# A state-space block with a token MLP on one core: norm sums on TensorE, a contiguous lag table, a fifth Strassen pair

## The chip, the cores and the metric

One core of one Trainium2 chip runs the whole kernel. The metric is the device time of one execution in microseconds, the median over several executions. The span in the profile is about 1.8 us shorter than that time. The granted clock is TensorE's clock as the profile shows it, as a share of full speed. Every run here compares with runs of the kernel before on the same chip in the same rounds; "ratio" is the mean time of one kernel's fast runs over the mean of the other's fast runs of those rounds, so it is not quite the ratio of the medians that stand beside it. The kernel before took 155.7 to 159.95 us on the chips used, most often 156 to 158.

## The reference, cut to what matters

```python
def reference(A_u, ..., B_w1, B_b1, B_w2, B_b2):          # x is 2048 tokens by 512 channels, bf16
    x = A_u
    h = x + ssm_conv(layernorm(x), ...)                    # a 2048-tap convolution for each channel
    # per channel: K[l] = Re sum_n C_n * exp(dt*A_n*l) * dt*B_n   (128 modes), y = K conv u + u*D
    return h + token_mlp(layernorm(h), B_w1, B_b1, B_w2, B_b2)
    # token_mlp: u = gelu(h^T @ w1 + b1)  (2048 -> 1792), y = u @ w2 + b2  (1792 -> 2048)
```

## The kernel before

The convolution is split at blocks of 128 tokens. The near part (inside a block and its neighbour) goes through a 64-point spectrum, `UF`. The far part goes through eight Chebyshev nodes for each block: **moments** `ms` of the normed x (a row for each block and node) are written to DRAM and read back as a table `Mb` of all shifts; the **far table** `G` holds the kernel at all lags between nodes; and the **lag product** multiplies the two, for each of 32 channel groups `s` and four quarters `q`. Its first call (O0) serves blocks 0 to 7, its second (O1) blocks 8 to 15. Each is 128 matmuls with 32-column weights.

```python
    def moments(self, hf):                       # hf = half of the blocks
        ...                                      # 8 matmuls into bank 3, then out with the norm's bias
        b.act(self.ms[r0:r0 + 64, :], self.bank(3, 0, D, r0, r0 + 64), AF.Identity, bias=self.mb[...])

    def far(self):                               # G is [P, 16, NJ, 32]: dims x, i (or j), s
        for i in range(0, NJ, 2):
            ...                                  # two matmuls fill two banks: (i, x, s)
            dst = self.G[:, :, i:i + 2].rearrange("p x i s -> p i x s")    # runs of 32 s side by side
            b.ts(dst, src, ...)  or  b.act(dst, src, AF.Copy)              # two on DVE, two on ACT

    def lag(self, hf):
        Gv = self.G[...].rearrange("p (q j) i s -> p q s (j i)", q=4)      # weights: one element every 64 bytes
        Mv = self.Mb[...].rearrange("p k (q j s) -> p q s k j", q=4, j=4)  # moving: likewise
        for s in range(32):
            for q in range(4):
                b.mm(self.ps[32*q:32*q+32, 32*s:32*s+32], Gv[:, q, s], Mv[:, q, s])
```

Behind O1 come the inverse transforms, the second norm and the token MLP, with four Strassen pairs in layer 1 (a pair forms two blocks of output columns with seven matrix products in place of eight). No order is written by hand: a list scheduler in the kernel file sets the order on each engine from a table of priorities, a cost for each instruction and an overlap test of the tiles that it reads and writes.

Other names in the text: an **eviction** copies a result from PSUM, where TensorE writes, to SBUF; `T` are eight products of exponentials and sines on DVE, from which TensorE forms samples of the convolution kernel; `kt` are the samples that G's matmuls read, `kf` those for the near part; `WL` and `nm` carry the weights and bias terms of the first norm; a y chunk is the inverse transforms and the far part of one block, which DVE adds to `X`; `H` is the second norm's output. The pitch is the time from one matmul's start to the next one's, and a filler is a matmul whose result nobody reads.

## Time and profile before

| | kernel before |
|---|---|
| time | 156.7 us (median) |
| span, granted TensorE clock | 154.7 us, 1.00 |
| first and second `ms` handed to the DMA | 26.9, 44.9 us |
| O0 starts, O1 starts | 44.6, 54.4 us |
| TensorE from O1 to its end | 97.9 us |

The groups of instructions, shapes apart, show what the change touches. A line has engine, operation, tiles, count, then busy us in all, the mean ns of one, and the engine's idle time ahead of it. (The 265 ns of one matmul overlap with those of its neighbours: 128 of them take 2.86 us.)

```profile
L499 PE MATMUL ps<-Mb,G 128*32 128x32 bf16 x256 | 5.7, 265 | 0.3 <-DMA Mb<-ms_scratch 0.3
...
L530 DVE TENSOR_SCALAR G<-ps 128x1024 bf16<-128x1024 f32 x2 | 2.4, 1217 | 0.0
...
L506 ACT ACTIVATE G<-ps 128x1024 bf16<-128x1024 f32 x2 | 1.9, 1020 | 0.0
...
L506 ACT ACTIVATE ms<-ps,mb 64x512 bf16<-64x512 f32 x2 | 1.4, 689 | 0.0
```

An eviction of 1024 elements to G takes 1.0 to 1.2 us, 1.0 to 1.2 ns an element, and one of `ms` (512) 0.69 us.

### The profile page before, as it was taken

To read this page: it belongs to the slowest core of one execution; us is meant where nothing else is said; L and a number is where in the kernel's file an instruction comes from. 1 tells how busy PE (TensorE), PEld (TensorE's weight loads), DVE (VectorE), ACT (ScalarE), POOL (GpSimd) and SP (SyncE) were. 2 spreads that over 40 slices of the span, in tenths; PEclk is the share of its full clock that TensorE was granted. 3 is DMA by queue.
4 is the path that set the end of the run, shared out by engine and by line. 5 is a ranking of instruction groups with operands and counts; after the bars stand their busy time and mean duration, and the time that the engine had idled before them with its cause. 6 is when DMAs were issued, how large, how long until landed. Compare 5 with 4: busy or idle time off the path is not lost.

```text
span 154.7 us, 3685 instructions
## 1 busy us (share of the span) xinstructions
PE 143.5 (93%) x1522; PEld 106.7 (69%) x1529; DVE 131.4 (85%) x308; ACT 78.2 (51%) x192; POOL 6.7 (4%) x11
## 2 busy tenths in 40 slices
PE   7849869989998889999999999999999999999993
PEld 3738753568565485545554788888888888888882
DVE  5099999998999998999999999957999994558663
ACT  4897999998997868614544832545320000000000
POOL 1590000000000000000000000000000000000000
PEclk9999999999999999999999999999999999999999
DMA  4899996266992508995590000000000101211123
GB/s 108 264 310 360 406 403 240 65 230 176 417 372 83 202 4 310 419 408 222 166 375 3 0 6 0 0 0 4 0 0 0 38 34 68 71 54 51 66 73 103
DMA packets 12351, 23.64 MB, mean 153 GB/s; under 512 B 1181, under 2 KB 8350, under 8 KB 12206
## 3 DMA queue, kind: packets, MB, share of 16 engines
q1 hardware_dynamic: 12190, 23.27, 41.8%
q8 instruction: 12, 0.20, 0.5%
q10 hardware_dynamic: 144, 0.13, 0.2%
q14 instruction: 5, 0.04, 0.1%
HBM read 21.17 MB, written 2.35 MB: 152 GB/s over the span
## 4 chain that ended last, share of the span: by engine, by line
PE 67%; DMA 14%; DVE 7%; SPq 5%; ACT 3%; issue 2%
PE ps L499 67%; DMA tab<-tables 8%; SPq L556 5%; DMA Mb<-ms_scratch 4%; DVE T L522 3%; DVE cmu L522 3%; DMA ms_scratch<-ms 2%; ACT G L506 1%; DVE ct L522 1%; ACT UF L506 1%; PE ps L784 1%; ACT ms L506 0%; ACT kf L506 0%; DVE X L536 0%; ACT mb L506 0%
## 5 line engine op out<-in xcount | busy, mean ns | idle before, releaser
L499 PE MATMUL ps<-H,W 128*128 128x512 bf16 (+1 forms) x180 | 32.5, 327 | 0.3 <-issue 0.2
L499 PEld LDWEIGHTS ps<-H,W 128*128 128x128 bf16 x184 | 17.7, 98 | 10.6 <-DVE H L532 0.2
L784 PE MATMUL ps<-idf 128*128 128x256 bf16 x162 | 22.0, 282 | 1.0 <-POOL idf L547 1.0
L499 PE MATMUL ps<-gT,W 128*128 128x256 bf16 x182 | 22.6, 273 | 0.0
L499 PEld LDWEIGHTS ps<-gT,W 128*128 128x128 bf16 x182 | 17.0, 98 | 3.0 <-DVE X L522 0.2
L784 PEld LDWEIGHTS ps<-idf 128*128 128x128 bf16 x162 | 15.6, 101 | 4.3 <-POOL idf L547 1.0
L522 DVE TENSOR_TENSOR W<-W 128x1024 bf16<-128x1024 bf16 (+1 forms) x23 | 14.9, 657 | 0.3 <-PE ps L499 0.2
L522 DVE TENSOR_TENSOR X<-ps,acc 128x256 bf16<-128x256 f32 x24 | 10.0, 422 | 5.5 <-PE ps L499 5.2
L499 PE MATMUL ps<-HT,W 128*128 128x256 bf16 x112 | 14.2, 273 | 0.0
L506 ACT ACTIVATE H<-X 128x512 bf16<-128x512 bf16 x16 | 10.0, 624 | 7.7 <-DVE X L536 7.7
L536 DVE SCALAR_TENSOR_TENSOR acc<-ps,b2T,X 128x256 f32<-128x256 f32 x24 | 11.1, 481 | 2.8 <-PE ps L499 2.2
L499 PEld LDWEIGHTS ps<-HT,W 128*128 128x128 bf16 x112 | 10.9, 98 | 1.4
L499 PE MATMUL ps<-TS,S 128*128 128x256 bf16 x84 | 11.6, 273 | 0.0
L499 PE MATMUL ps<-TS,W 128*128 128x256 bf16 x84 | 11.3, 273 | 0.0
L536 DVE SCALAR_TENSOR_TENSOR X<-ps,X 128x512 bf16<-128x512 f32 x16 | 10.6, 687 | 0.2 <-PE ps L499 0.2
L506 ACT ACTIVATE gT<-snap,b1T 128x256 bf16<-128x256 f32 x12 | 6.0, 505 | 9.1 <-DVE snap L522 9.1
L542 DVE BATCH_NORM_STATS2 st<-X 128x6 f32<-128x512 bf16 x12 | 7.4, 679 | 3.5 <-DMA X<-in_A_u_dram 3.5
L506 ACT ACTIVATE UF<-ps,ub 128x512 bf16<-128x512 f32 x16 | 10.2, 686 | 0.2 <-PE ps L499 0.2
L499 PEld LDWEIGHTS ps<-TS,S 128*128 128x128 bf16 x84 | 7.9, 98 | 1.4 <-DVE acc L536 0.4
L499 PEld LDWEIGHTS ps<-TS,W 128*128 128x128 bf16 x84 | 8.2, 98 | 1.0
L506 ACT ACTIVATE gT<-ps,b1T 128x512 bf16<-128x512 f32 (+1 forms) x10 | 5.4, 606 | 4.7 <-PE ps L499 4.7
L499 PEld LDWEIGHTS ps<-O,tab 128*128 128x128 bf16 x64 | 4.8, 98 | 3.9 <-DVE O L530 0.8
(127 smaller groups left out, 233.4 us busy)
## 6 DMA issues: line engine op xcount, KB each, us to landing
W<-in_B_w_dram SPq DMA_DIRECT2D x4, 1792.0 KB, 10.9
W<-in_B_w_dram SPq DMA_DIRECT2D x2, 2048.0 KB, 9.3
W<-in_B_w_dram SPq DMA_DIRECT2D x2, 1536.0 KB, 7.9
Mb<-ms_scratch SPq DMA_DIRECT2D x2, 1024.0 KB, 6.0
out_dram<-X SPq DMA_DIRECT2D x15, 128.0 KB, 1.7
tab<-tables SPq DMA_DIRECT2D x1, 1296.0 KB, 13.1
X<-in_A_u_dram SPq DMA_DIRECT2D x4, 256.0 KB, 4.7
X<-in_A_u_dram SPq DMA_DIRECT2D x2, 512.0 KB, 11.8
```

The lines of the kernel that those rows point to most:

```text
L499: return self.r.add("pe", lambda e: e.matmul(out, lhsT=lhsT, rhs=rhs, start=start, stop=stop, skip_group_check=onto), [lhsT, rhs], [out], ...
L506: return self.r.add("act", lambda e: e.activation(out=out, in_=in_, func=func, bias=bias, scale=scale, accum_out=accum_out), [in_, bias, s ...
L522: return self.r.add(eng, lambda e: e.tensor_tensor(out=out, in0=a, in1=b, op=op), [a, b], [out], self._d(eng, nel(out), m), **k)
L536: return self.r.add(eng, lambda e: e.scalar_tensor_tensor(out=out, in0=a, scalar=s, in1=b, op0=op0, op1=op1, accum_out=accum_out), [a, s, ...
L542: return self.r.add("dve", lambda e: e.bn_stats(out=out, in_=a), [a], [out], 67 + nel(a) / 0.96, **k)
L556: return self.r.add(eng, lambda e: e.dma_start(out=out, in_=in_), [in_], [out], max(by / RATE.get(out.tensor.name.split("_")[0], 410) + 0. ...
L784: self.rec.hot = (hot, lambda e, bk: e.matmul(self.bank(bk, 0, 256), lhsT=hv[:, 0:P], rhs=hv[:, :], start=True, stop=True))
```

## The change

The intent: take the first norm's statistics off DVE (TensorE forms x·x and the row sums from transposed loads of x), put each set of 32 weights of the lag product side by side, work G off in two halves so that O0 can start on the first, save TensorE time by a fifth Strassen pair, and move the scaling of the DFT weights to ACT. All priorities are new. The core of the diff, with cuts:

```diff
-        self.G = take("G", [P, 16, NJ, 32], BF16)
+        self.G = take("G", [P, 2, 16, 16, NJ], BF16)           # half, s, x, j
 def far(self):
+        for h in range(2):
+            for c in range(0, 4, 2):
 ...
-            dst = self.G[:, :, i:i + 2].rearrange("p x i s -> p i x s")
+                    dst = self.G[:, h, :, :, 2*(c+q):2*(c+q)+2].rearrange("p s x i -> p i x s")
+                    src = self.bank(bb + q).rearrange("p (i x s) -> p i x s", i=2, x=16)
+                    # odd ones on DVE, even ones on ACT, 512 elements each
 def lag(self, hf):
-        Gv = self.G[...].rearrange("p (q j) i s -> p q s (j i)", q=4)
-        Mv = self.Mb[...].rearrange("p k (q j s) -> p q s k j", q=4, j=4)
+        Gv = self.G[...].rearrange("p h s (q j) i -> p h q s (j i)", q=4)
+        Mv = self.Mb[...].rearrange("p k (q s j) -> p q s k j", q=4, j=4)
 def moments(self, hf):
-        b.act(self.ms[r0:r0+64, :], self.bank(3, 0, D, r0, r0+64), ...)
+        b.act(self.ms[r0:r0+64, :].rearrange("p (q s j) -> p q j s", q=4, j=4),
+              self.bank(3, 0, D, r0, r0+64).rearrange("p (q j s) -> p q j s", q=4, j=4), ...)
+def stats(self, hf):             # in place of BN_STATS on DVE
+        for k in range(8):       # Gram blocks of 32 tokens: t^T t for 4 channel chunks
+            ... b.mm(self.bank(bk, ...), t, t, ...)
+        ...                      # row sums against a column of ones; mask and reduce on DVE
 def loads(self):
-        ... x in six pieces, W1's quarters 0 and 1 early
+        for h in range(2):
+            ld(17 + h, self.XT[:, h], self.x_in[0][...], transpose=True)
+            ld(8 + h, self.X[:, 8*h:8*h+8], xv[:, 8*h:8*h+8])
+PAIRS = [(6, 10), (7, 11), (8, 12), (9, 13), (4, 5)]           # fifth Strassen pair
+FA = (0,)                                                      # first half's DFT weights scaled on ACT
```

## The prediction

> **What bounds the kernel now.** I read the chain in order of time first: it says which wait ends last at each point.
>
> ```profile
> 9.19 12.65 DMA tab<-tables
> ...
> 25.82 3.68 DVE T L522 x5
> ...
> 39.85 0.34 PE ps L499 x2
> 40.19 0.02 issue
> 40.21 1.94 ACT G L506 x2
> ...
> 44.22 0.70 ACT ms L506
> 44.91 0.02 issue
> 44.93 3.14 DMA ms_scratch<-ms
> 48.07 0.02 issue
> 48.09 6.31 DMA Mb<-ms_scratch
> 54.40 0.04 issue
> 54.44 2.85 PE ps L499 x114
> ...
> 81.83 70.49 PE ps L499 x621
> ```
>
> The columns are start, length and what. Up to 54.4 us the kernel is a chain of latencies: parameters and the T products on DVE, samples and the far table G, then the second half of the moments through DRAM (3.1 us out, 6.3 us back). From 54.4 to 152.3 nothing but TensorE is on it. The busy table by stretches confirms it and shows the second danger:
>
> ```profile
> core 0: us, PE busy (x) PEld busy (x) DVE busy (x) ACT busy (x) POOL busy (x), PEclk, DMA share, GB/s
> ...
> 45.00:54.40 9.40, 7.93 (x158) 5.14 (x152) 9.12 (x20) 7.68 (x20) 0.00 (x0) 1.00 0.49 165
> ...
> 60.00:70.00 10.00, 9.95 (x58) 5.05 (x58) 9.77 (x25) 4.39 (x16) 0.00 (x0) 1.00 1.02 414
> 70.00:82.00 12.00, 11.89 (x77) 6.78 (x78) 11.70 (x30) 6.38 (x20) 0.00 (x0) 1.00 0.63 234
> 82.00:94.00 12.00, 12.00 (x92) 8.90 (x91) 11.59 (x32) 6.14 (x13) 0.00 (x0) 1.00 0.01 3
> ```
>
> From 60 to 94 us TensorE has no gap, but DVE has under 3% left too. So the end is the start of the second lag product (O1, 54.44) plus TensorE's work after it. That work can be counted from the program, with the pitches of the trace (217 ns a 512-column matmul, 109 ns a 256-column one, from runs of 24 in 5.4 us and of 28 in 3.06 us): O1 2.85, twelve y chunks of 0.65, 96 matmuls of the plain half of layer 1 20.8, four Strassen pairs of 56 x 109 ns 24.4, layer 2 (392 x 109 ns) 42.7; sum 98.5. 54.4 + 98.5 = 152.9 against 152.3 seen. The last DVE addition and the output DMA add 2.4 us to the span (154.7), and the time is 1.8 us over the span (156.5 for the profiled run).
>
> **What the Trainium skill says.** "TensorE: Matmul & The Clock Gate", section Back-to-back issue gap: N/2.4 + 2.5 ns warm, 109 ns for 256 columns; the trace agrees. Its section on the 56 ns gap puts a floor of about 25 ns on the start-to-start of small matmuls; the lag product, column-packed, runs 128 in 2.86 us, 22.3 ns each, so the measurement decides. "SBUF — State Buffer", section Door 1, gives 16-byte lines that a stride should stay within; G's weights stand 64 bytes apart now, and 22.3 ns against 13.3 ns of streaming 32 columns at 2.4 GHz is compatible, though not shown to be due to it. "DMA: Bandwidth & Descriptors", section Latency and other measured facts, gives a crossbar transpose 261 GB/s with a non-contiguous middle dimension, 350 to 400 contiguous. No run before shows a transpose; 1 MB is then an estimated 3 to 4 us.
>
> **The change, part by part.**
>
> Norm 1. Removed: 12 BN_STATS at 0.61 us pitch (7.3 us of DVE) and four ACT pairs (5.6 us between 29.7 and 36.6). Added: two transposed loads ahead of x itself, 128 small matmuls and 32 one-column sums for each half, and on DVE a masking pass and a reduction (0.4 us each, twice). The first half's BN_STATS ran at 7.5 to 12.4 us, and m waited behind them, while its own inputs (CX, written at 9.13) were ready by about 9.9. In the new order ACT reaches the sines earlier (square moved behind the table load): I get the last sine at 16.5 us instead of 17.3. DVE's list from SN to the last T is SN 0.74, q 0.6, mask and reduction 0.8, the complex products 8.0 and eight T's of 0.735: about 16. So T ends near 32.3 instead of 35.1: 2.8 us won. Condition: the first transpose is in by about 12 us (0.8 MB of parameters first, done near 6.5, then 4 us, then latency), so that the Gram matmuls end by 17.5 at the cold clock.
>
> G and the order behind T. This is where I see the gain spent. The retuned order puts WL, nm (the norm's bias terms) and the second half's reduction after the last T. The bias, hence every UF eviction and the first moments, waits for them, and bank 5 is shared by the second half's sums and half of the samples. In order: T 32.3; nm 33.5; bias on ACT 34.5; the moments' matmuls 35.6; UF, exponential, UF, ms to 36.6 (0.57 us each with bias); the other samples on PE to 38.5; select 40.4; kt 41; then G. Before, T to kt took 39.1 - 35.1 = 4.0 us, now some 8.5, seven of which are ACT evictions that before ran at 23 to 30 us. G's evictions alternate ACT and DVE but each waits for the one before in the same half (their write ranges interleave): 4 x 0.75. G's first half is ready at 44.5. The moments arrive too: ms 36.6, out 2, back 5.6 (the first pair in the trace: issue 26.88, 28.82): 44.3. O0 therefore starts at about 44.5, against 44.57: **nothing is won up to here**.
>
> The lag product. Contiguous weights: I take 16 ns for 22.3: 0.8 us a half.
>
> O0 to O1. The half of Mb that does not depend on the second ms is fetched early, so the last fetch is 0.5 MB: 3.8 us estimated for 6.3. ms1 comes after O's eight evictions on ACT (2.3), y0, a bias, a UF, an H square: 6 us after O0 starts, at 50.5 to 51. 51 + 2 + 3.8 = 57 for **O1, 2.5 us later than before**. In return eight y chunks and three inverse transforms are done by then, instead of four.
>
> TensorE after O1. Counting the new program: O1 2.0, y 4.6, 64 plain matmuls 13.9, five pairs 30.5 (a pair costs 6.1 for 6.94 plain, so the fifth saves 0.84), layer 2 42.7: 93.7 to 95. Saved: 4.0.
>
> DVE after O1. Added: four sums for the fifth pair (4 x 0.6) and three additions (3 x 0.35), 3.5 us, in a stretch that has 1.1 us left. Three more X and one more product are done earlier (3 us), so it is near a draw. Laying the two orders side by side, H10 to H12 come about 1 us after TensorE wants them; the others just in time. W1's last quarter, now issued behind the moments, lands near 70, and the fifth pair's sums are due at 73.
>
> Sum: 57 + 94.2 + 1 + 2.4 = 154.6 us of span, 156.4 of time. The chain up to here errs on the late side if ACT's order has slack that I charge in full, and all priorities were searched anew for this program, so I shade it by 1.8 us: **154.6 us**.
>
> **Rivals.** First: the norm was the bound, and what leaves DVE is time won. 10 us of DVE (BN, Fs, four O evictions) less 7 added would give 3 us, with the 4 us of TensorE work some 150. For it: DVE is full from 12 us on. Against it: after T the chain runs through ACT and DMA, and DVE stands idle at about 36 to 40. Second: the transpose is slow. At 150 GB/s the first half lands at 14, the Gram sums end at 20 and DVE, in order, stands still 2 us: 158. For it: nothing in the trace; the skill's two figures differ by 50%. Third: DVE becomes the bound behind O1, since the plain matmuls that filled TensorE's waits fall from 20.8 to 13.9 us; 2 to 3 us of gaps, 158. Against it: DVE's 12 us of idle after 120. Fourth: G's writes, now scattered two bytes at a time at 256-byte steps, evict slower; each 0.1 us costs 0.4 before O0.
>
> **Range and chances.** Front and O1 time are uncertain by some 3 us, the rest by 1.5. 80%: 151 to 158.5. Faster by over 2% (under 153.6) needs O1 before 55.5 or so: 0.38. Slower by over 2% (over 159.8) needs a slow transpose as well as gaps: 0.07. Else the same: 0.55.
>
> **What would show it.** In the changed profile: last T near 32, kt near 41, O0 near 44.5, O1 near 57, TensorE busy about 94 of the 95 to 96 us after it, the lag product under 18 ns a matmul, transposes landing by 12 and 16. I am wrong if kt comes within 5 us of T (then the first rival holds), if DVE waits at the mask for the Gram sums, or if TensorE shows over 2 us of gaps between O1 and 110.

## The result, and the profile after

The changed kernel took **174.19 us** (173.55 to 174.80, four fast runs) against 156.7 (156.29 to 157.68): ratio 1.1105, 95% interval 1.1038 to 1.1173, slower. The prediction's range ended at 158.5.

The chain of waits of the changed kernel, in order of time (start, length, what), from the T products to the start of O0:

```profile
27.98 5.88 DVE T L529 x8
...
41.73 0.87 PE ps L506 x17
42.60 0.02 issue
42.62 0.60 ACT kf L513
43.22 2.32 ACT G L513
45.55 0.02 issue
45.57 2.42 DVE G L537
47.99 0.02 issue
48.02 2.44 ACT G L513
50.45 0.02 issue
50.48 2.49 DVE G L537
52.97 0.01 DVEq L471
52.98 0.05 issue
53.02 2.42 DVE G L537
```

The T products end at 33.9 for 32.3 in my walk, and kt starts at 41.7 for 41. Then G alone holds the chain for twelve microseconds, to 55.4: ACT, DVE, ACT, DVE for the first half, each of 512 elements and 2.3 to 2.5 us long, each waiting for the one before, and a fifth behind them on DVE. (The bytes of two evictions do not overlap. The overlap test works with ranges, and in the new layout the ranges of one half lie within each other, so the scheduler sets a wait.) The groups, shapes apart, say the same of all eight, and of the other parts of the new layout:

```profile
L537 DVE TENSOR_SCALAR G<-ps 128x512 bf16<-128x512 f32 x4 | 9.7, 2435 | 1.5 <-ACT G L513 1.5
L513 ACT ACTIVATE G<-ps 128x512 bf16<-128x512 f32 x4 | 9.6, 2529 | 0.2 <-DVE G L537 0.2
...
L513 ACT ACTIVATE ms<-ps,mb 64x512 bf16<-64x512 f32 x2 | 2.8, 1398 | 0.1
L506 PE MATMUL ps<-Mb,G 128*32 128x32 bf16 x256 | 2.8, 190 | 2.8 <-DVE G L537 2.8
```

Half the elements take twice the time: 4.8 ns an element on DVE and 4.9 on ACT for G (2435 and 2529 over 512), 2.7 for `ms`. The lag product itself is twice as fast (2.8 us for 5.7).

The busy table by stretches, for three of those shown before (same columns as there):

```profile
45.00:54.40 9.40, 5.20 (x84) 2.29 (x84) 8.62 (x4) 8.31 (x7) 0.00 (x0) 0.61 0.87 251
...
60.00:70.00 10.00, 8.79 (x55) 4.23 (x51) 6.36 (x18) 8.62 (x22) 0.00 (x0) 0.80 0.41 93
...
82.00:94.00 12.00, 9.45 (x59) 5.25 (x57) 11.02 (x28) 3.55 (x16) 0.00 (x0) 0.89 1.03 409
```

In 45 to 54.4 us DVE is busy for 8.62 us with four instructions, and ACT for 8.31 with seven. TensorE had 158 matmuls there and has 84; its granted clock falls to 0.61. From 82 to 94, where it had no gap before, 2.55 us are lost.

Three distances carry the comparison: O0 starts at 53.0 for 44.6 (+8.5), from O0 to O1 there are 17.9 us for 9.9, from O1 to TensorE's end 99.5 for 97.9. Against my walk (44.5, 12.5, 95.2) these are +8.5, +5.4 and +4.3, which add up to the difference between the 172.7 us of span and the 154.6 that I had before shading.

### The profile page after: what moved, and what is told of

It is laid out like the page before. It is cut to its first block, busy times and chain, and to the rows that moved or that the text cites. A ratio compares the mean times of both kernels' runs of the same rounds, so it can differ in the third digit from the quotient of the medians.

```text
span 172.7 us, 4201 instructions
## 1 busy us (share of the span) xinstructions
PE 145.6 (84%) x1789; PEld 105.6 (61%) x1789; DVE 135.7 (79%) x300; ACT 85.2 (49%) x190; POOL 6.9 (4%) x11
## 4 chain that ended last, share of the span: by engine, by line
PE 55%; DVE 23%; ACT 13%; POOL 3%; DMA 2%; issue 1%; POOLq 1%; SPq 0%; DVEq 0%
PE ps L506 55%; DVE G L537 4%; DVE T L529 3%; DVE cmu L529 3%; ACT UF L513 3%; ACT G L513 3%; POOL bc L529 2%; ACT SC L513 2%; DMA raw<-in_A_B_re_dram 2%; DVE S L529 2%; DVE X L543 1%; DVE Pb L529 1%; DVE ct L529 1%; ACT O L513 1%; DVE acc L543 1%
## 5 line engine op out<-in xcount | busy, mean ns | idle before, releaser
L506 PE MATMUL ps<-H,W 128*128 128x256 bf16 (+1 forms) x168 | 30.2, 325 | 2.5 <-DVE H L539 1.6
L506 PEld LDWEIGHTS ps<-H,W 128*128 128x128 bf16 x168 | 16.6, 101 | 11.5 <-DVE H L539 2.1
L506 PE MATMUL ps<-HT,W 128*128 128x256 bf16 x128 | 15.9, 273 | 0.0
L506 PEld LDWEIGHTS ps<-HT,W 128*128 128x128 bf16 x128 | 12.5, 98 | 1.5
L791 PE MATMUL ps<-idf 128*128 128x256 bf16 x70 | 11.7, 321 | 0.0
L513 ACT ACTIVATE snap<-ps 128x256 f32<-128x256 f32 x15 | 5.4, 385 | 11.8 <-PE ps L506 11.7
L537 DVE TENSOR_SCALAR G<-ps 128x512 bf16<-128x512 f32 x4 | 9.7, 2435 | 1.5 <-ACT G L513 1.5
L791 PEld LDWEIGHTS ps<-idf 128*128 128x128 bf16 x70 | 7.4, 113 | 4.0 <-issue 2.5
L513 ACT ACTIVATE G<-ps 128x512 bf16<-128x512 f32 x4 | 9.6, 2529 | 0.2 <-DVE G L537 0.2
L513 ACT ACTIVATE gT<-snap,b1T 128x256 bf16<-128x256 f32 x15 | 7.2, 503 | 4.9 <-DVE snap L529 4.8
```

The costliest lines, as they stand in the source:

```text
L506: return self.r.add("pe", lambda e: e.matmul(out, lhsT=lhsT, rhs=rhs, start=start, stop=stop, skip_group_check=onto), [lhsT, rhs], [out], ...
L513: return self.r.add("act", lambda e: e.activation(out=out, in_=in_, func=func, bias=bias, scale=scale, accum_out=accum_out), [in_, bias, s ...
L537: f = lambda e: e.tensor_scalar(out=out, in0=a, scalar1=s1, scalar2=None, op0=op0)
L791: self.rec.hot = (hot, lambda e, bk: e.matmul(self.bank(bk, 0, 256), lhsT=hv[:, 0:P], rhs=hv[:, :], start=True, stop=True))
```

## The experiments

My theory after reading the trace: the two-byte writes of G, 256 bytes apart, are the main loss; the rest is what follows from it (the cold clock) and the late moments. The rivals: the serial order of the evictions, the transposes, DVE behind O1, or the added operations as such. Sixteen kernels ran, all with correct results, on several chips; the kernel before ran beside each. Where the order is said to be kept, and in the walked runs, the traces show the same sequence of instructions on every engine, but for a few matmul records that a trace misses.

### G with s contiguous again (same order, same waits)

```diff
-        self.G = take("G", [P, 2, 16, 16, NJ], BF16)
+        self.G = take("G", [P, 2, 16, NJ, 16], BF16)
-  dst = self.G[:, h, :, :, 2*(c+q):2*(c+q)+2].rearrange("p s x i -> p i x s")
+  dst = self.G[:, h, :, 2*(c+q):2*(c+q)+2, :].rearrange("p x i s -> p i x s")   # + the old waits, kept by hand
-  Gv = ... "p h s (q j) i -> p h q s (j i)"
+  Gv = ... "p h (q j) i s -> p h q s (j i)"
```

> The changed kernel with one thing undone: G is stored with s contiguous, so its eight evictions write runs of 32 bytes, and the lag product's weights stand 32 bytes apart again. The order on every engine and every wait are the same as in the changed kernel. Theory A (the scattered two-byte writes of G are the main cause): an eviction takes 0.6 to 0.8 us instead of 2.45, the first lag product starts near 45.5 instead of 53.0, TensorE does not cool, and the time falls to 160 to 165 us. If the contiguous weights are what halved the lag product's pitch, it goes back from 11 to 20 ns or more. Theory B (the slow transpose or a DVE bound behind O1 costs the time, and G's wait would only have been spent elsewhere): 171 us or more. Theory C (the evictions are slow for another reason than where they write, for example their serial order): they stay above 2 us and the time stays at 174.

Measured: 166.19 us, ratio 1.0601 [1.0518, 1.0684]. The groups of this run:

```profile
L506 PE MATMUL ps<-Mb,G 128*32 128x32 bf16 x256 | 4.6, 216 | 1.2 <-DMA Mb<-ms_scratch 1.2
...
L537 DVE TENSOR_SCALAR G<-ps 128x512 bf16<-128x512 f32 x4 | 2.7, 690 | 0.1
L513 ACT ACTIVATE G<-ps 128x512 bf16<-128x512 f32 x4 | 2.4, 596 | 0.7 <-DVE G L537 0.5 <-PE ps L506 0.2
```

Evictions fall to 0.60 and 0.69 us in the same serial order, so where they write is the cost, not their order. Eight of the 17.5 us come back, and the time ends 1.2 us above the 160 to 165 that I expected: O0 starts at 48.2, not 45.5, because it now waits for the first moments. The lag product's pitch goes back to 17 or 18 ns, not to 20 or more.

### The same writes, but no false waits between them

```diff
-    while rest and ... and len(bases) * rest[0][1] <= 64:
+    while rest and ... and len(bases) * rest[0][1] <= 256:     # overlap test exact for G; the order changes too
```

> The changed kernel with the scattered writes of G kept, but with the overlap test made exact, so that the evictions of one half no longer wait for each other and ACT and DVE may evict side by side; the order of the program changes too, since the scheduler sees other waits. Theory A: each eviction still takes 2.4 us or more, two run at a time, the first half of G needs about 5 us instead of 10, and the time falls to 167 to 171. If the serial order alone was the cause (theory C): evictions shorten to under 1.5 us. Theory B: 174 as before.

Measured: 169.63 us, ratio 1.0834 [1.0752, 1.0916]. Evictions stay at 2.46 and 2.67 us, now side by side. Two engines at once win back about 4 us (0.0271 of the ratio), and the reordering that came with it (O0 at 55.0, in fact later than in the changed kernel, O1 at 65.9) makes this only a bound. The serial order is not the cause of the long evictions.

### Moments in the plain layout (same order, same waits)

```diff
-  b.act(self.ms[...].rearrange("p (q s j) -> p q j s"), self.bank(3, ...).rearrange("p (q j s) -> p q j s"), ...)
+  b.act(self.ms[...], self.bank(3, ...), ...)
-  Mv = ... "p k (q s j) -> p q s k j"
+  Mv = ... "p k (q j s) -> p q s k j"
```

> The changed kernel with the layout of the moments undone: ms is written as it comes out of the bank (contiguous) and the lag product reads it with j 64 bytes apart; order and waits as in the changed kernel. Theory A: each of the two ms evictions goes from 1.40 to about 0.7 us, both sit on the path, so the time falls by 0.7 to 1.4 us, to about 173. If the contiguous moving operand, and not the contiguous weights, halved the lag product's pitch, it goes back from 11 to about 22 ns, and half of the gain is lost.

Measured: 173.75 us, ratio 1.1061 [1.0962, 1.1159], against 1.1105 for the changed kernel: a gain of the expected sign that the interval does not separate from none.

```profile
L506 PE MATMUL ps<-Mb,G 128*32 128x32 bf16 x256 | 4.7, 240 | 2.4 <-DVE G L537 2.4
...
L513 ACT ACTIVATE ms<-ps,mb 64x512 bf16<-64x512 f32 x2 | 1.4, 678 | 0.0
```

With the run before last this is a clean pair: weights contiguous alone 4.7 us, moving operand contiguous alone 4.6, both 2.6 to 2.8, neither 5.7 (in the kernel before, where the weights stand 64 bytes apart; in the run before last 32). The lag product needs both operands side by side for its full speed.

### The same layout, walked in the order of memory

```diff
-  dst = self.G[...].rearrange("p s x i -> p i x s")
-  src = self.bank(bb + q).rearrange("p (i x s) -> p i x s", i=2, x=16)
+  dst = self.G[...]                                              # s, x, i
+  src = self.bank(bb + q).rearrange("p (i x s) -> p s x i", i=2, x=16)
```

> The changed kernel with G in the same place and layout, but each eviction walks its tile in the order s, x, i instead of i, x, s: pairs of two bytes side by side, then steps of 16 bytes, while the PSUM side is read with a stride. Order, waits and number of elements are the same. Theory A (the size of the write step sets the cost: 256-byte steps 4.8 ns an element, the ms eviction with its 8-byte steps 2.7): an eviction takes 1.0 to 1.6 us, the first lag product starts near 48 and the time is 164 to 169 with the lag product still at 11 ns. If two-byte pieces as such are the cost, whatever their distance: 2 us or more and over 171.

Measured: 165.72 us, ratio 1.0567 [1.0475, 1.0659]. The bytes in G are the same as in the changed kernel, and only the order in which an eviction visits them differs; the strided side is now PSUM:

```profile
L537 DVE TENSOR_SCALAR G<-ps 128x512 bf16<-128x512 f32 x4 | 2.7, 689 | 0.2 <-ACT G L513 0.2
L506 PE MATMUL ps<-Mb,G 128*32 128x32 bf16 x256 | 2.6, 187 | 1.5 <-DMA Mb<-ms_scratch 1.5
L513 ACT ACTIVATE G<-ps 128x512 bf16<-128x512 f32 x4 | 2.5, 634 | 0.6 <-DVE G L537 0.4
```

An eviction is as cheap as in the contiguous layout, cheaper than my estimate of 1.0 to 1.6, and the lag product keeps its 10 ns. So the fast weights never needed slow evictions.

### Pairs, but as far apart as before

```diff
-  dst = self.G[...].rearrange("p s x i -> p i x s")
-  src = self.bank(bb + q).rearrange("p (i x s) -> p i x s", i=2, x=16)
+  dst = self.G[...].rearrange("p s x i -> p x s i")
+  src = self.bank(bb + q).rearrange("p (i x s) -> p x s i", i=2, x=16)
```

> The changed kernel with G's layout, order and waits as they are, each eviction walked x, s, i: the two-byte elements now go out in pairs (four bytes side by side), but from pair to pair the address still jumps 256 bytes, as it did from element to element. It parts the two things that the walked run (s, x, i: pairs, then 16-byte steps, 0.63 and 0.69 us) had changed at once. If the single two-byte element is the cost and pairs at any distance are cheap: 0.65 to 0.75 us an eviction and 165 to 166.5 us. If the distance is the cost: half of the scattered price or more, 1.2 to 2.5 us an eviction, and 168 to 174.

Measured: 164.82 us, ratio 1.0488 [1.0422, 1.0555].

```profile
L537 DVE TENSOR_SCALAR G<-ps 128x512 bf16<-128x512 f32 x4 | 2.8, 694 | 0.2
...
L513 ACT ACTIVATE G<-ps 128x512 bf16<-128x512 f32 x4 | 2.6, 650 | 0.6 <-DVE G L537 0.4
```

Jumps of 256 bytes cost nothing when two elements of two bytes go out together. So the cost comes with the single two-byte element. Among single elements the distance seems to count as well: 4.8 to 4.9 ns at 256 bytes for G, 2.7 at 8 bytes for `ms`; but `ms` has 64 partitions for 128, and no run changes the distance alone.

### That part alone, in the kernel before (same order)

```diff
-        self.G = take("G", [P, 16, NJ, 32], BF16)
+        self.G = take("G", [P, 32, 16, NJ], BF16)
-  dst = self.G[:, :, i:i + 2].rearrange("p x i s -> p i x s")
+  dst = self.G[:, :, :, i:i + 2].rearrange("p s x i -> p i x s")
 ...                     # Gv to match; the overlap test's limit raised, which keeps the old order
```

> The kernel before, with one part of the change alone: G is stored as 32-column weights side by side (order s, x, j), each of its four evictions of 1024 elements walking i, x, s as before and so writing two bytes at a time at 256-byte steps. The order on every engine is that of the kernel before. Theory A (the scattered writes cost 4.8 ns an element): an eviction takes 4.7 to 5.0 us instead of 1.0 to 1.2; ACT's two end near 50 instead of 42.2, which pushes the second ms, and with it O1, from 54.4 to about 62; the time becomes 162 to 166 us. The lag product alone gains at most half of what both contiguous operands gave: 18 ns a matmul. Theory B (the rest of the new order costs the time, not this part): 156 to 158.

Measured: 166.89 us, ratio 1.0672 [1.0625, 1.0719], a little over the range.

```profile
L530 DVE TENSOR_SCALAR G<-ps 128x1024 bf16<-128x1024 f32 x2 | 9.4, 4704 | 4.0 <-PE ps L499 4.0
L506 ACT ACTIVATE G<-ps 128x1024 bf16<-128x1024 f32 x2 | 9.3, 4892 | 0.0
```

The loss travels with this one edit: O0 starts at 55.4 (44.6 before), the second `ms` goes out at 53.7 (44.9), O1 starts at 65.0 (54.4), and what follows O1 is as long as before (97.7 us). Nothing of the norm, the transposes or the Strassen pair is in this kernel.

### Both operands of the lag product contiguous, in the kernel before (same order)

```diff
+  dst = self.G[:, :, :, i:i + 2]                # G as [P, 32, 16, NJ], walked in memory order
+  src = ....rearrange("p (i x s) -> p s x i", i=2, x=16)
+  b.act(self.ms[...].rearrange("p (q s j) -> p q s j"), self.bank(3, ...).rearrange("p (q j s) -> p q s j"), ...)
 ...                     # Gv and Mv to match; the overlap test's limit raised, as above
```

> The kernel before, with the lag product's operands both made contiguous (G in the order s, x, j, its evictions walked in memory order; ms written with j innermost, as the changed kernel does), nothing else, same order on every engine. Theory A: G's evictions stay at 1.0 to 1.3 us, the lag product runs at 10 to 11 ns a matmul instead of 22, so the second one takes 1.4 us instead of 2.85; the slower ms eviction (1.40 for 0.69) gives back 0.7: 155.3 to 156.5 us, ratio 0.99 to 1.0. If the lag product's pitch was not on the path: no change, or 0.7 slower.

The expectation describes the kernel wrongly in one point: its `ms` eviction is walked in memory order as well, and took 0.75 us, not 1.40. Measured: 157.05 us for 156.47, ratio 1.0011 [0.9959, 1.0064]. The lag product falls from 2.86 to 1.23 us for 128 matmuls (9.6 ns each), and nothing of the 1.6 us of O1 is seen in the time. (Its profile fell in a slow run, so where it went is left open. That profile gives a hint: from O1 to TensorE's end it has 97.7 us for 97.9, and in the first 27.2 of them TensorE stands still for 1.6 us and DVE for 0.6, against 0.3 and 1.0 of 27.4 in the kernel before.) This part of the change is worth nothing that half a per cent would show.

### TensorE kept warm through the wait for G

```diff
+        at = first lag matmul;  out[at:at] = 76 fillers          # first try
+        57 fillers in five gaps: 15 + 8 + 7 + 13 + 14            # second try
```

> The changed kernel, scattered evictions and all, with 76 more filler matmuls (256 columns, into a bank that is free) set before the first lag product, so that TensorE works through the wait for G instead of standing still from 44 to 53 us. Nothing else moves. The theory gives the slow clock of 47 to 65 us (granted 0.5) a share of the loss: the matmuls of 54 to 65 us would take 0.38 instead of 0.61 us each, the second ms would come 1.5 to 3 us sooner, and the time falls to 171 to 173. If the evictions alone made the loss, and TensorE's clock only filled time in which it waited anyway: 174 as before, within 0.5.

Measured: 179.30 us (177.94 to 182.05), ratio 1.1374 [1.1263, 1.1485]. A failed experiment: the fillers ran from 52.5 to 64.0 us, until 58 at half clock, in front of a lag product that was ready (profile slow), so it tells nothing of the clock. The second try:

> The changed kernel, scattered evictions and all, with 57 more filler matmuls placed in the gaps in which TensorE waits for an eviction of G (15, 8, 7, 13 and 14 of them, each lot a little shorter than its gap at full clock), unlike the run with 76 in one lot, which began at half clock at 52.5 us and ended at 64, nine microseconds too late. Theory: O0 starts near 53 as in the changed kernel, the clock stays at full through 65 us, the stretch from O0 to O1 falls from 17.9 to 14 or 15 us (14.4 with the walked evictions), and the time is 170.5 to 172.5: the cold clock is worth 2 to 4 us of the 17.5. If it is worth nothing: 174. If the fillers run late again: O0 after 54, and over 173, and then it tells nothing of the clock.

Measured: 173.38 us, ratio 1.1004 [1.0942, 1.1067]. O0 starts at 53.4, and from 54.4 to 65 us the granted clock is 1.00 instead of 0.54. In that stretch TensorE does its work in 7.60 busy us for 8.82, but O0 to O1 shortens only from 17.9 to 16.9. From O1 to TensorE's end there are 98.1 us for 99.5; the clock from 82 to 94 us is 1.00 there, 0.89 in the changed kernel. So the cold clock is worth about 1 us before O1 and 1.6 in all (0.0101 of the ratio; the two intervals overlap, so the ratios do not part it from nothing), less than the 2 to 4 expected. What made O0 to O1 long is in the chain above: the second half's last eviction ends at 55.4, 2.5 us after the first lag product starts, and everything behind it, `ms` too, follows that.

### Moments walked in memory order as well

```diff
-  b.act(self.ms[...] "p q j s", self.bank(3, ...) "p q j s")
+  b.act(self.ms[...] "p q s j", self.bank(3, ...) "p q s j")       # on top of the walked G
```

> The changed kernel with the walked evictions of G, and the ms eviction walked in the order of its memory as well (read strided from PSUM, written contiguously); layout, order and waits as before. An ms eviction goes from 1.40 to about 0.7 us; both are on the path in that kernel (first ms to Mb to O0, second ms to Mb to O1), so about 1.3 us less than 165.7: 164 to 165, with the lag product still at 10 to 11 ns a matmul.

Measured: 163.74 us, ratio 1.0465 [1.0416, 1.0513], a gain over 1.0567 that the intervals do not part from none. An `ms` eviction takes 0.68 us, O0 starts at 46.4 (47.8), O1 at 60.6 (62.2). Repaired twice, the changed kernel is still 7 us slower than the one before.

### The norm ahead of the T products

```diff
+PRIO.update({'wl0:dve': -5, 'mom0:act': -3, 'lns1:dve': -5, ...})   # on top of the walked G: priorities alone
```

> The changed kernel with the walked evictions of the run before last (165.7 us), and with the priorities of the norm alone changed: sums, weights, bias and moments of both halves go ahead of the cmu and T products on DVE (WL, nm) and ahead of the samples on TensorE and ACT. The theory: after G is mended, O0 (47.8) waits for the first moments (ms written out at 38.4, back at 47.7), which wait for WL and nm behind the last T at 33.9, and O1 (63) waits for the second (ms at 54.7); in the kernel before the first were out at 26.9, the second at 44.9. Then ms0 is out by 28 to 30, O0 starts when G is there (43 to 46), ms1 is out by 45 to 48, O1 starts by 54 to 57, and the time falls to 156.5 to 160. The rival (DVE's total load before G and behind O1 sets the time, and moving the norm ahead only moves T back by as much): O0 no earlier than 47, and 163 or more.

Measured: 167.50 us, ratio 1.0698 [1.06, 1.0797]; two of its four runs were slow. The profiled fast run, 164.37 us, has these lines in its chain:

```profile
48.13 1.40 ACT ms L514
49.55 3.52 DMA ms_scratch<-ms
53.09 4.74 DMA Mb<-ms_scratch
57.83 0.04 issue
57.87 0.68 PE ps L507 x56
```

The wait is as I said: the first `ms` goes out at 30.2 for 38.4, the second at 49.5 for 54.8, and O1 starts at 57.9 for 62.2. The time does not follow: from O1 to TensorE's end it is 102.3 us for 99.2. Until 70 us TensorE is busy for 8.9 of 12.1 us, and from 70 to 110 DVE is busy for 39.8 of 40. Whether that comes of the other priorities, made for another order, or of DVE's load as such is not shown: of the rival, the time of 163 or more came true, and the last T does end later (36.3 for 33.1), but O0 starts at 46.4, before its 47. A single move shows the wait, not what it is worth.

### All priorities searched again

```diff
-PRIO = {'G0:act': 18.2, ...}
+PRIO = {...}                          # searched with the scheduler's own model
-    while ... <= 64:                  # exact overlap test
+    while ... <= 256:
+  ....cost += 130                     # evictions of G as long as measured
+  avail[e] = t0 + 4400 for a transpose   # third and fourth search only: a transpose holds SyncE
```

These edits are on top of walked G and `ms`. Four results ran.

> The changed kernel with walked evictions of G and ms, an exact overlap test (so that the evictions of a half need not wait for each other) and all priorities searched again for this program. The order then puts the first half's norm before the T products and the first ms out near 29 us (37.6 in the run with walked evictions of both), the second near 44 (53.6). Theory: what was left of the loss after G was mended is the order in which the new program brings the moments, not the operations that the change added. Then O0 starts at 43 to 46, O1 at 50 to 54 (63 in the changed kernel with walked G), TensorE needs 94 to 98 us behind it, and the time is 150 to 156 us, faster than the kernel before. The rival (the added operations themselves, the transpose, the Gram sums, the fifth pair, cost what is left): 160 or more, whatever the order.

Measured: 158.55 us for 157.82, ratio 1.0050 [0.9972, 1.0127], profile slow.

> The same program as the run before it with another result of the same search: first ms near 28, second near 43, O0 at 44 to 46, O1 at 50 to 54. Theory: 150 to 156 us, within 2 us of the run before it. The rival: 160 or more.

Measured: 159.10 us, ratio 1.0124 [1.0056, 1.0192]. Neither meets its range. The model had the first `ms` at 28 to 29 us; it went out at 34.1 and 30.4. The second transpose, put behind x, held SyncE for 7.2 and 7.5 us, which the model took for 0.5, and DVE's mask waited 4.6 and 1.0 us for the Gram sums. (The first of the two profiles is slow.) The rival, 160 or more whatever the order, did not come true in either.

> As the two runs with searched priorities, but the search now knows that SyncE is held some 4.4 us by the issue of each transpose and that it lands later; in the first of those two runs the second transpose was put behind x, held SyncE 7.2 us and its Gram sums started at 21.8. Theory (the order in front is what is left): the first ms is out by 28 to 30, the second by 43 to 46, O0 at 43 to 46, O1 at 49 to 53, 95 to 97 us of TensorE behind it: 150 to 156 us. The rival (the front of the new program cannot be as early as that of the kernel before, because the transposes and the sums on TensorE come on top): O1 at 56 or later and 157 or more.

Measured: **155.37 us** (154.73 to 156.43, six fast runs) for 157.63, ratio **0.9862** [0.9815, 0.9909]. This version beats both kernels, the one before by 1.4%. Its second transpose held SyncE for 7.1 us too, but nothing on DVE waited for it. Its chain at the same place:

```profile
43.90 0.69 ACT ms L513
44.59 0.02 issue
44.60 2.62 DMA ms_scratch<-ms
47.22 0.02 issue
47.24 6.53 DMA Mb<-ms_scratch
53.76 0.04 issue
53.81 0.67 PE ps L506 x50
```

The first `ms` is out at 30.1, O0 starts at 45.6, O1 at 53.8 (my theory said by 53), and TensorE needs 97.0 us from there.

> The same program as the run before it, with another result of the same search, which keeps the second moments' return later (O1 modelled 6 us later). Theory: O1 at 55 to 57, 153 to 158 us; in both, O1's start and the end should differ by 95 to 98 us.

Measured: 161.87 us, ratio 1.0232 [1.0171, 1.0293]. O1 starts at 63.5 in its (slow) profile, later than its model and its range; 95.9 us follow. The same instructions in another order cost 5.8 us more than in the run before it (0.0370 of the ratio).

### More fillers in the best version

```diff
-            if start[i] < WARM[0]:      # fill from 20 us
+            if start[i] < FILL:         # fill from 13.5 us
```

> The best kernel so far (155.37 us with searched priorities) with 18 filler matmuls instead of 5 in TensorE's wait for the second transpose (15 to 20 us); everything else in the same order. In that kernel the clock is at half from 19 to 38 us, and the chain from 22.7 to 41 runs over TensorE. Theory: at full clock the moments' and the samples' matmuls there take half as long, the first ms comes 1 to 2 us sooner, kt about 1 us, and the time falls by 0.5 to 2 us, to 153.5 to 155. If DVE and the DMA set that stretch: the same as before, 155.4. If the fillers outlast the wait: slower.

Measured: 156.70 us, ratio 0.9964 [0.9906, 1.0022]. Fifteen fillers ran by 17.1, then TensorE stood still for 3.6 us all the same, and the clock was at half from about 22 to 36 us (18 to 35 in the best version). The fillers bought nothing, and whether a warm front would help is left open. The run is also the only second look at the best order, on another chip: its ratio is 1% higher, and the two intervals only just meet. Whether the fillers cost that, or the gain of 1.4% is smaller than it looked, is not shown.

## Why the prediction was wrong

| profiled run | first, second `ms` out | O0 | O1 | O1 to TensorE's end | span |
|---|---|---|---|---|---|
| before | 26.9, 44.9 | 44.6 | 54.4 | 97.9 | 154.7 |
| my walk | 36.6, 51 | 44.5 | 57 | 95.2 | 154.6 |
| changed | 38.5, 63.1 | 53.0 | 70.9 | 99.5 | 172.7 |
| + G walked | 38.4, 54.8 | 47.8 | 62.2 | 99.2 | 163.8 |
| + `ms` walked | 37.6, 53.6 | 46.4 | 60.6 | 98.5 | 161.5 |
| + searched order (155.37 us) | 30.1, 44.6 | 45.6 | 53.8 | 97.0 | 153.2 |

**G and the order behind T.** This is the step that failed: "4 x 0.75". The form was right, since the four of a half do wait for each other, and the place was right, since this is where the gain was spent. The size was wrong: 0.75 us was taken from evictions that write 64 bytes in a row, and those that write single two-byte elements took 2.45 us. I saw the difference and put it last among the rivals: "evict slower; each 0.1 us costs 0.4 before O0". At 1.7 us too little, that sentence gives 6.8 us; 8.5 were seen at O0. I had looked up the line rule of SBUF for the weights, where the change improves it, and did not hold it against the writes, where the same change breaks it. The prediction's chance of 0.07 for "slower" was built on a slow transpose, not on this. From 1.1105 to 1.0567 in the ratio, 8.4 of the 17.5 us, come back with a different walk of the same tile; alone in the kernel before, the scattered writes cost 10.5 us (1.0672).

**What hung on it, and was not in the prediction at this place:** TensorE's clock. With TensorE idle in front of G it was at half from 47 to 64 us, and with fillers in those gaps it stayed at full. The second warm run puts that at 1 to 1.6 us, inside the 8.4.

**The moments.** "ms 36.6, out 2, back 5.6: 44.3" was short by three terms: T was later by 1.6 us (half of it since the last sine came at 17.3, as before, and not at 16.5), the `ms` eviction took 1.40 us where the walk has 0.57 (single two-byte elements again, here 8 bytes apart), and the way back took 7.3. With G repaired O0 waits for them at 47.8. Walking `ms` brings 0.0102 of the ratio, 1.6 us, within the intervals.

**O0 to O1.** I took 51 for the second `ms` and 3.8 us for half a megabyte. With G repaired they were 54.8, of which 3.3 are O0's own delay, and 5.4.

**TensorE after O1.** The counted work was right: 95.9 and 96.0 us in two of the re-ordered runs and 97.0 in the best, for 93.7 to 95 and one of gaps (the profiles of the first two are slow). In the changed kernel it is 99.5. I had named over 2 us of gaps before 110 as a sign of being wrong, and there are 2.55 us between 82 and 94 alone. The third rival said DVE; I read the trace as order more than load, which no run parts. With G walked, 22 matmuls of the fifth pair ran ahead of the last y chunks, so the last X products, and DVE's work that TensorE then waited for, came late.

**The premise that "all priorities were searched anew for this program"**, with which I shaded the number down, was an assumption. Searched for a program with cheap evictions, the best order gives 0.9862 instead of 1.0465, about 9 us; the other three results gave 1.0050, 1.0124 and 1.0232, which is 4 to 7 us. That is the second half of the loss (7.3 us were left after both walks), and it is shown for the set of three edits together (order, exact overlap test, corrected costs), not for each. The same search was not run on the chip for the kernel before.

**What held.** From T to kt it was 7.9 us against "some 8.5", so by the sign that I had set the first rival (the norm was the bound, 150 us) is out. That kt came within 0.7 us of the walk is in part luck: T was 1.6 later and the stretch behind it 0.8 shorter. DVE did not wait for the Gram sums: the mask ran right behind q, at 18.67. The lag product went below 18 ns, at 10.9, and was worth no more than the little I gave it: in the kernel before, nothing that shows. The transposes landed at about 12 and 17 us (7.2 and 8.0 us after their issue), close to the 12 and 16 asked for, so the second rival, at 158, did not happen in the changed kernel; in a re-ordered run it did, for the second half (7.2 us on SyncE, DVE waiting 4.6 us for the sums).

## What to carry to other kernels

When a layout is turned round so that one reader finds its operands side by side, price the writer again, from a row that writes in that pattern; and try first to keep the layout and change the order in which the writer walks it, so that at least two two-byte elements go out together and the stride falls on the PSUM side. A scheduler that costs an instruction by its element count will not see such a thing, and an order made for wrong costs can hide a gain as large as the one sought: measure, correct the costs, and search again before a change is judged.

## What the Trainium skill lacked or had wrong

- "Vector Engine (DVE) Microarchitecture Reference", section Measured stream behaviour on trn2, has the writes in 4-byte words: 1.71 ns a column for a destination that hops with every element, up to 2.5 in its worst row, and no charge for hops between runs of two adjacent words. For single two-byte elements at steps of 256 bytes the runs here show more: 4.76 ns an element on DVE (2435 over 512) and 4.94 on ACT (2529). Two adjacent two-byte elements, four bytes in all, were already enough for the full rate at jumps of 256 bytes (0.69 us for 512). I had not read this section before predicting.
- "SBUF — State Buffer", section Door 1, asks for at least two hits in a 16-byte line. Pairs agree with it. Single elements 8 bytes apart, two to a line, do not: the `ms` eviction took 1.40 us so and 0.68 in memory order. It has no figure for an eviction that misses.
- "PSUM — Partial Sum Buffer" warns that a non-contiguous pattern slows matmuls. No page has that an eviction's strided read from PSUM costs next to nothing here: 0.63 us on ACT with the source 1024 bytes apart from element to element, 0.60 in runs.
- "TensorE: Matmul & The Clock Gate", section on the 56 ns gap, gives no less than about 25 ns from start to start, and does not except packed matmuls there (its own part on packing has some 4 ns between tiles). Column-packed 32-column matmuls ran at 9.6 ns with both operands contiguous, 17 to 18 with one, 22.3 with neither; no page has figures of the pitch by the operands' strides.
- "DMA: Bandwidth & Descriptors" gives a transpose's bandwidth. It has no time for which the issue of one of this size holds SyncE: 4.4 us for 1 MB in the changed kernel (4397 and 4473 ns), and 7.1 to 7.5 us in the four runs in which x was queued right ahead of it. If that is the transfer, 1.05 MB in 4.0 to 4.7 us (every transpose without x ahead) is an estimated 220 to 260 GB/s, at or below its 261.
